# Attention in five batches a unit: a third tile of maxima in the banks of the products with v, and moved copies, squares and statistics

## Chip, cores and metric

The kernel runs on one core of a Trainium2 chip. The metric is the device time of one execution in microseconds (us). TensorE (PE in the profile, PEld for its weight loads), VectorE (DVE), ScalarE (ACT), GpSimd (POOL) and SyncE (SP, which here only issues DMAs) each work through a queue of their own and wait for each other through semaphores. Products land in PSUM, 8 banks of 128 x 512 f32.

## What is computed

```
xn = layernorm(x)                                   # x: 2048 x 512
q, k, v = split(xn @ wqkv)                          # 32 heads of 16
scores = q k^T * 16**-0.5, where 0 <= i - j < 256, else -1e9
s = (softmax(scores) v) @ wo                        # 512 x 512
g = silu((silu(xn @ w1) * (xn @ w3)) @ w2)          # w1, w3: 512 x 1792, w2: 1792 x 512
out = x + s * g
```

All data are f32. The large products are made from f16 halves, high and low, in three products each (high high, high low, low high), so each operand must first be scaled by a power of two and cut in two.

## The kernel before

**Work.** Tokens go in four tiles of 512 (`t`), heads in four groups of eight (`g`). A *unit* is four heads of one group in one tile: 4 x 4 x 2 = 32 units, in the order of `t`, `g`, `p`. The dense work, `gate_up` (L839) and `down` (L884) over 14 slices of the feed-forward weights for each tile, projections of q and k (L534), values (L504) and the final product with wo (`total`, L926), is cut into pieces of mostly 6 matmuls of 128 x 128 x 512.

**Attention.** For each unit `pass1` (L572) makes 8 tiles of scores whose row maxima are reduced on VectorE (products L588, reduction L600). It runs two units ahead, because the maxima, turned by two small products (L615), go out through DRAM into two extra rows of q (L623, L625). `pass2` (L641) makes the scores again, transposed and with the maxima taken off: 4 chunks a unit in the first tile of tokens (`FIRST`), 5 in the others (`CHUNKS`). A chunk is 8 to 12 small products (L662) into a tile `s` of two banks, one or more additions of a mask on VectorE (L669), and one exponential on ScalarE (L672) into a tile `pt`, of which there are four buffers. `values` multiplies chunks with v into the tile `po` (L690). After the last chunk `finish` reads `po` out with a ScalarE copy (L700) and a VectorE addition (L703), and sends the halves out by DMA; the second unit of a pair calls `normalise` (L723): reciprocals go through DRAM, `invert` multiplies on GpSimd, `cut` copies on ScalarE (L743) and subtracts on GpSimd. All small products of attention use quarters or eighths of TensorE side by side.

**PSUM.** Two banks are `m0`, `m1` for dense work, four are two tiles `s` (pool `pss`), two are the one tile `po` (pool `pso`).

**Order.** TensorE runs in the order of the program, written out by hand. The other engines' order is made by the framework from priorities and a model of time. `batches` (L1025) takes a unit's tiles alternately from `pass2` and `pass1`, two to a *batch*, an odd one carried to the next unit; the products with v of a chunk group (`cuts`) are issued at the end of the batch after the one with its last scores (`late`). `spread` (L1063) issues a batch, then dense pieces until their share of the unit's cost is reached; a group of products with v counts as `COLS` = 2.5 matmuls a chunk. `step` counts batches and dense pieces; `later(n, f)` places `f` n steps on. `besides` are small extra products (sums of squares for the scales, transposes of the next x) that ride on a tile of maxima, at most one or two a batch; `beside_scores(n, f)` queues one.

**Preparation.** Weights are read as f32, their squares summed (`squares`, L222: ScalarE L231 or VectorE L233) and cast (L243), summed over partitions by `powers` on TensorE, then cut: `split` (L293) uses a ScalarE copy (L294) and a VectorE subtraction (L295), `split_pool` (L302) two ScalarE copies (L303, L304) and two halves of a GpSimd subtraction (L300). `measure` (L773) does this for two slices of the feed-forward weights, `weights` (L311) for wv and wo. `prepare_beside` (L478) loads the next x, takes its statistics (L406, L407), the reciprocal root (`rstd`) and centres it.

Of the kernel before, what the change touches and what calls it, by code (L numbers as in the profile page):

```python
# [21 lines left out]
P = 128  # L22
# [56 lines left out]
def tile_block(ctx: ExitStack, tc: tile.TileContext, x, wqkv, wo, w1, w3, w2, out):  # L79
# [59 lines left out]
    def later(n, f):  # L139
        made_so_far[0] += 1  # L140
        queue.append((now[0] + n, made_so_far[0], f))
# [80 lines left out]
    def squares(parts, on_act=0, apart=0):  # L222


        ssq = small.tile([P, len(parts)], F32, name="ssq")

        def one(i, raw):

            sq = ppool.tile([P, D], BF16, name="sqa" if i < on_act else "junk", bufs=1)
            if i < on_act:  # L230
                nc.scalar.activation(sq, raw, AF.Square, accum_out=ssq[:, i:i + 1])  # L231
            else:
                nc.vector.tensor_tensor_reduce(out=sq, in0=raw, in1=raw, scale=1.0, scalar=0.0,  # L233
                                               op0=ALU.mult, op1=ALU.add, accum_out=ssq[:, i:i + 1])
        for i, raw in enumerate(parts):
            if apart:
                later(apart * (i // 2 + 1), lambda i=i, raw=raw: one(i, raw))
            else:
                one(i, raw)
        sb = small.tile([P, len(parts)], BF16, name="sb")  # L240

        def cast():
            nc.vector.tensor_copy(sb, ssq)  # L243
        if apart:
            later(apart * (len(parts) + 1) // 2, cast)
        else:
            cast()
        return sb
# [62 lines left out]
    def weights(name, w):  # L311

        cell = {}

        def load():
            cell["raw"] = [take(F32) for _ in range(NC)]
            for c, raw in enumerate(cell["raw"]):
                nc.sync.dma_start(raw, w[c * P:(c + 1) * P, :])

        def norm(apart=0):  # L320
            cell["sb"] = squares(cell["raw"], on_act=2 * (name == "wv"), apart=apart)

        def scale(s=None):
            p2 = const.tile([P, 1], F32, name=f"p2{name}")
            inv = const.tile([P, 1], F32, name=f"inv{name}")

            def rest():
                cell["p2"], cell["inv"], cell["sw"] = p2, inv, scaled(inv, WS, f"sw{name}")
            return then(s, powers(cell["sb"], 1, p2, inv, s), rest)

        def cut(apart=0):
            if name == "wo":

                made = [take(F16) for _ in range(NC)]
                hi, lo = ([m[:, k * D:(k + 1) * D] for m in made] for k in range(2))
            else:
                both = [const.tile([P, NC, D], F16, name=f"{name}{k}") for k in "hl"]
                hi, lo = ([b[:, c, :] for c in range(NC)] for b in both)

            def one(c, raw):  # L340
                split(hi[c], lo[c], raw, cell["sw"])
                give(raw)
            for c, raw in enumerate(cell["raw"]):
                if apart:
                    later(apart * c, lambda c=c, raw=raw: one(c, raw))
                else:
# [131 lines left out]
    def prepare_beside(t, more=0):  # L478


        load, stats, rstd, centre, turn = prepare(t)
        made = [(0, lambda b=b: load(b)) for b in range(4)]
        for b in range(4):
            made.append((0, lambda b=b: later(more + 8 + b, lambda: stats(b))))
        made.append((0, lambda: later(more + 12, lambda: rstd(0, 4))))
        for b in range(4):
            made.append((0, lambda b=b: later(more + 13 + b, lambda: centre(b))))
        return made, lambda: besides.extend(lambda s, b=b, n=n: turn(b, n, s) for b in range(4) for n in (0, 2))

    def value(j, scores_bank=False):  # L490
# [81 lines left out]
    def pass1(t, g, p):  # L572
# [3 lines left out]
        whole = NM[(2 * (t * NG + g) + p) % len(NM)]  # L576
        nm = whole[:, 0:32].rearrange("p (b i) -> p b i", b=2)

        def part(ii, a):
            qa, ka = QA[t, g], keys(t, g)  # L580
            i = t * 4 + ii
            n, mask = ((i + 1) * P, M1.rearrange("p a b -> p (a b)")[:, (1 - i) * P:]) if i < 2 else (WIN, MW)
            s = scores_bank()
            for c in range(2):
                e = (ii + 3) * P if i < 2 else (ii + 2) * P + 64 * (c + 1)
                for r in range(2):
# [24 lines left out]
        def finish(s):  # L611
# [13 lines left out]
                    nc.sync.dma_start(qa[64 * r + KR:64 * r + KR + 2, 2 * p:2 * p + 2, :].rearrange("p a q -> p (a q)"),  # L625
                                      dm.rearrange("(b r i) q -> r b (i q)", b=2, r=2)[r])
            return rest
        return [lambda ii=ii, a=a: part(ii, a) for ii in range(4) for a in range(2)]

    def last_maxima():  # L630
        s = scores_bank()
# [6 lines left out]
    OT = {}  # L638
    ON = {}

    def pass2(t, g, p, cuts):  # L641

        es = WQK[g][2]
        cell = {}
# [70 lines left out]
            values(*cs)  # L715
            finish()
        n = len(chunks)
        cols = [None] * n
        for cs in cuts:
            cols[cs[-1]] = len(cs), lambda cs=cs: (last if cs[-1] == n - 1 else values)(*cs)  # L720
        return [lambda c=c: scores(c) for c in range(n)], cols

    def normalise(t, g):  # L723
        on, dd = ON.pop((t, g))
        dr = small.tile([P, 32], F32, name="dr")
        nc.sync.dma_start(dr, dd.rearrange("h (b c) -> (h b) c", c=32))
# [12 lines left out]

        def cut():  # L740
            OT[t, g] = made = take(F16)
            O[t, g] = o = made.rearrange("p (a q) -> p a q", a=2)
            nc.scalar.copy(o[:, 0, :], on)  # L743
            halves(nc.gpsimd.tensor_sub, o[:, 1, :], on, o[:, 0, :])
        later(8, invert)
        later(18, cut)

# [25 lines left out]
    def measure(f, apart=0):  # L773
# [25 lines left out]
                for k in range(2):  # L799
                    later((1, 2, 4, 6)[2 * i + k], lambda i=i, k=k: cut(i, k))  # L800
        if started:
            beside_scores(4, scale)
        else:
            later(9 if apart else 6, scale)

    def measure_down(k):

# [154 lines left out]
    def feed_forward():  # L962
# [3 lines left out]
        for t in range(NT):  # L966
            for f in range(FB):
                if t == 0:
                    if f % 2 or f == 0:
                        pieces += [(0, lambda f=f: load(0, f)) for f in (range(f + LEAD, min(f + LEAD + 2, FB)) if f else range(4, LEAD + 1))]  # L970
                    elif 0 < f < FB - 2:
                        pieces.append((0, lambda f=f + 2: measure(f, 1)))
                    pieces += [(0, lambda k=k: measure_down(k)) for k, (_, f1) in enumerate(GROUPS) if f == f1 - 1]
                else:
                    if f == 0:
# [42 lines left out]
            done[0] += made[-1][0]  # L1018
        return made

    late = []
    late_cost = [0]
    carried = []

    def batches(n, u, ahead):  # L1025


        rows1 = pass1(*ahead) if ahead else []
        rows2, cols2 = [], []
        if u:  # L1030
            cuts = ((0, 1), (2, 3)) if u[0] == 0 else ((0, 1, 2), (3, 4)) if ahead else ((0, 1), (2, 3), (4,))
            rows2, cols2 = pass2(*u, cuts)
        order = carried[:]
        carried.clear()
        if u and not ahead and maxima:
            order.append((last_maxima, None, 1))
        for k in range(max(len(rows1), len(rows2))):
            order += [(f, c, 0) for f, c in zip(rows2[k:k + 1], cols2[k:k + 1])]
            order += [(f, None, 1) for f in rows1[k:k + 1]]
        if len(order) % 2 and n < len(units) - 1:  # L1040
            carried.append(order.pop())
        pairs = [order[k:k + 2] for k in range(0, len(order), 2)]
        made = []
        due = late_cost[0]
        for pair in pairs:

            pair.sort(key=lambda x: x[2])

            def batch(pair=pair):
                alone[0] = True  # L1050
                for f, _, _ in pair:
                    f()
                ready = late[:]
                late.clear()
                late.extend(c[1] for _, c, _ in pair if c)
                for c in ready:
                    c()
            made.append((due, batch))
            due = sum(COLS * c[0] for _, c, _ in pair if c)
        late_cost[0] = due  # L1060
        return made

    def spread(made, dense):  # L1063
# [136 lines left out]
    want = EARLY  # L1200
    for n, u in enumerate(units):
        if n == 1:
            first, second = prepare_beside(1, 6)
            run(first)
            later(26, second)
        if n == 6:
# [10 lines left out]
        k = n // 2 + 2  # L1217
        if n % 2 == 0 and k < len(tiles):
            later(1, lambda k=k: fetch(*tiles[k]))
    while late:  # L1220
        ready = late[:]
        late[:] = []
        for c in ready:
            c()
        step()
    for b in range(2):
        residual(NT - 1, b)
    run(ffn)
# [31 lines left out]
```

## Time and profile before

| | |
|---|---|
| median of 3 runs | 875.03 us (872.63 to 876.66) |
| the profiled execution | 873.85 us |
| its span, first to last instruction | 872.1 us |
| mean granted TensorE clock | 0.988 |
| TensorE busy | 833.8 us |
| VectorE busy | 607.7 us |
| ScalarE busy | 407.4 us |
| GpSimd busy | 192.4 us |

A row of a group reads: line, engine, operation, tile written <- tiles read, shapes, count, busy time, mean ns of one, idle time before them and what ended most of it. A row of the order of time reads: start, length, engine, line, operation, tiles, shapes, count, and in brackets the idle time of the engine before it with what ended it. Matmuls overlap and their ends are modelled, so intervals between their starts say more than their lengths.

### The profile page before, as it was taken

The page shows a single profiled execution, that of the slowest core. Times are in us where ns is not written, and L with a number is a line of the kernel's source. Part 1 is how long each engine was busy: PE and PEld are TensorE (multiplying, and loading weights), DVE is VectorE, ACT ScalarE, POOL GpSimd, SP SyncE. Part 2 cuts the span into 40 slices and gives each one's busy share as a digit, 9 for nine tenths or more (in the row PEclk, how much of TensorE's full clock was granted, in tenths as well). Part 3 has the DMA queues.
Part 4 walks back from the last instruction along what each step waited for, and adds up shares of the span by engine and source line. Part 5 has one row for each costly group of instructions (what it writes and reads, how often), then busy time and mean ns, then how long its engine had stood idle before and what let it go on. Part 6 is the DMA issues. An engine that isn't in the chain of part 4 may idle for free.

```text
span 872.1 us, 22496 instructions
## 1 busy us (share of the span) xinstructions
PE 833.8 (96%) x8734; PEld 376.8 (43%) x8734; DVE 607.7 (70%) x2017; ACT 407.4 (47%) x594; POOL 192.4 (22%) x317
## 2 busy tenths in 40 slices
PE   9898989979999999999999999999999999999997
PEld 4343434434444444444444444444444444444443
DVE  8686767946797667796768775777676776566435
ACT  6897967372424444334343444343434444342521
POOL 2254338160111203111111211121111113131211
PEclk9999999998999999999999999999999999999999
DMA  9967625335633434452433344344443263433102
GB/s 290 280 209 237 206 81 161 110 108 142 200 107 89 129 95 125 115 171 78 137 106 92 123 112 131 117 116 105 128 128 94 69 152 87 130 94 101 49 9 61
DMA packets 95323, 110.62 MB, mean 127 GB/s; under 512 B 17200, under 2 KB 60528, under 8 KB 95216
## 3 DMA queue, kind: packets, MB, share of 16 engines
q1 hardware_dynamic: 94928, 108.67, 42.6%
q8 instruction: 68, 1.11, 0.6%
q10 hardware_dynamic: 288, 0.52, 0.2%
q14 instruction: 39, 0.32, 0.1%
HBM read 76.28 MB, written 28.57 MB: 120 GB/s over the span
## 4 chain that ended last, share of the span: by engine, by line
PE 71%; DVE 11%; ACT 6%; DMA 5%; issue 4%; POOL 1%; SPq 1%; POOLq 0%; ACTq 0%; DVEq 0%
PE m L839 26%; PE m L884 13%; PE po L690 8%; PE m L534 7%; PE s L662 5%; PE s L588 4%; PE m L504 4%; PE m L926 4%; DVE junk L600 3%; ACT pt L672 2%; DVE s L669 2%; DMA slot<-in_B_w_dram 1%; ACT slot L303 1%; DMA dQ<-slot 1%; ACT sqa L231 1%
## 5 line engine op out<-in xcount | busy, mean ns | idle before, releaser
L672 ACT ACTIVATE pt<-s,es 128x1024 f32<-128x1024 f32 x152 | 168.7, 1112 | 225.6 <-DVE s L669 208.8
L839 PE MATMUL m<-XH,slot 128*128 128x512 f16 x896 | 267.7, 380 | 0.4 <-DVE slot L854 0.2
L300 POOL TENSOR_TENSOR slot<-slot,slot 128x256 f16<-128x256 f32 (+1 forms) x220 | 144.0, 680 | 518.1 <-ACT slot L863 381.5
L600 DVE CUSTOM_DVE_ANT_0 junk<-s,MW 128x320 bf16<-128x320 f32 x448 | 217.3, 485 | 33.6 <-PE s L588 21.0
L839 PEld LDWEIGHTS <-slot 128*128 128x128 f16 x1344 | 123.0, 98 | 154.4 <-issue 15.6
L669 DVE TENSOR_TENSOR s<-s,MK 128x256 f32<-128x256 f32 (+2 forms) x280 | 121.3, 435 | 73.5 <-PE s L662 70.5
L839 PE MATMUL m<-XL,slot 128*128 128x512 f16 x448 | 169.8, 379 | 0.0
L884 PE MATMUL m<-slot,slot 128*128 128x512 f16 x672 | 158.2, 384 | 2.3 <-DVE slot L854 2.0
L884 PEld LDWEIGHTS <-slot 128*128 128x128 f16 x672 | 62.0, 98 | 81.5 <-issue 12.2
L588 PE MATMUL s<-KA,qa 48*64 48x320 f16 (+2 forms) x1024 | 73.2, 299 | 23.4 <-ACT pt L672 13.4
L690 PE MATMUL po<-pt,V 64*32 64x320 f32 (+4 forms) x2880 | 87.0, 350 | 0.0
L662 PE MATMUL s<-qa,KA 50*64 50x320 f16 (+3 forms) x1472 | 62.2, 261 | 3.2 <-DVE M L600 1.6
L690 PEld LDWEIGHTS po<-pt,V 64*32 64x32 f32 x2880 | 48.2, 107 | 29.9 <-issue 9.4
L662 PEld LDWEIGHTS <-KA 50*64 50x64 f16 x1472 | 31.7, 105 | 67.5 <-issue 42.4
L863 ACT CAST slot<-slot 128x512 f16<-128x512 f32 x56 | 34.5, 616 | 53.5 <-DVE slot L859 53.1
L850 ACT ACTIVATE slot<-m,sgs 128x512 f32<-128x512 f32 x56 | 38.2, 683 | 45.0 <-PE m L839 43.7
L854 DVE SCALAR_TENSOR_TENSOR slot<-slot,m 128x512 f32<-128x512 f32 x56 | 38.3, 684 | 27.5 <-ACT slot L850 27.0
L859 DVE SCALAR_TENSOR_TENSOR slot<-m,slot 128x512 f32<-128x512 f32 x56 | 38.5, 687 | 21.5 <-PE m L839 21.3
L588 PEld LDWEIGHTS <-qa 48*64 48x64 f16 x1024 | 29.2, 106 | 53.6 <-issue 29.1
L300 POOL TENSOR_TENSOR on<-on,rb 128x256 f32<-128x256 f32 x32 | 22.6, 727 | 129.2 <-DMA dm<-mt 40.7
L900 DVE SCALAR_TENSOR_TENSOR slot<-m,dsc,slot 128x512 f32<-128x512 f32 x48 | 35.8, 746 | 18.4 <-PE m L884 18.0
L534 PE MATMUL m<-XH,whi 128*128 128x512 f16 x120 | 45.6, 388 | 0.0
(143 smaller groups left out, 832.6 us busy)
## 6 DMA issues: line engine op xcount, KB each, us to landing
slot<-dW SPq DMA_DIRECT2D x126, 256.0 KB
slot<-in_B_w_dram SPq DMA_DIRECT2D x42, 256.0 KB
dW<-slot SPq DMA_DIRECT2D x42, 256.0 KB
slot<-in_A_x_dram SPq DMA_DIRECT2D x30, 256.0 KB
KA<-dK SPq DMA_DIRECT2D x24, 288.0 KB
qa<-dQ SPq DMA_DIRECT2D x32, 192.0 KB
dK<-slot SPq DMA_DIRECT2D x16, 256.0 KB
dQ<-slot SPq DMA_DIRECT2D x16, 256.0 KB
```

The source lines that it names most:

```text
L300: op(out[:, c], a[:, c], b[:, c])
L534: nc.tensor.matmul(cell["pp"], a[:, k, c, :], b[:, c, :], start=(c, i) == parts[0][0], stop=(c, i) == parts[-1][-1])
L588: nc.tensor.matmul(s[64 * c:64 * c + 64, r, :n], qa[rows, 2 * p + a, ii * P + 64 * c:ii * P + 64 * c + 64], ka[rows, 2 * p + a, e - n:e], ...
L600: nc.vector.tensor_tensor_reduce(out=junk[:, :n], in0=s[:, r, :n], in1=mask, scale=1.0, scalar=NEG, op0=ALU.add, op1=ALU.max, accum_out=M[ ...
L662: nc.tensor.matmul(s[64 * h:64 * h + 64, r, o:o + 64 * n], ka[rows, 2 * p + a, 64 * (m + 4):64 * (m + 5)], qa[rows, 2 * p + a, 64 * (m + k ...
L669: nc.vector.tensor_add(v, v, MK[:, kind, of:of + n, :].unsqueeze(1).to_broadcast([P, 2 * len(which), n, 64]))
L672: nc.scalar.activation(pt, s, AF.Exp, scale=es)
L690: nc.tensor.matmul(cell["po"][32 * i:32 * i + 32, h, 64 * (m + k):64 * (m + k + n)], V[64 * h:64 * h + 64, (4 * t + m // 2) % VB, hd * VW: ...
L839: nc.tensor.matmul(cell[k], w[:, (a * NC + c) * P:(a * NC + c + 1) * P], b[:, c, :], start=c == 0 and i == 0, stop=c == NC - 1 and i == 2)
L854: nc.vector.scalar_tensor_tensor(sg, sg, 1.0, cell[0], op0=ALU.add, op1=ALU.mult)
L859: nc.vector.scalar_tensor_tensor(sg, cell[1], 0.5 * HS / (WS * XS)**2, sg, op0=ALU.mult, op1=ALU.mult)
L884: nc.tensor.matmul(ps, hh[:, a * TW + b * P:a * TW + (b + 1) * P], w[:, c * D:(c + 1) * D], start=f == f0 and i == 0, stop=f == f1 - 1 and ...
```

## The change

- `batches` no longer pairs tiles. A written plan gives each unit its batches: `W` is a chunk of scores, `M` a tile of maxima in a tile `s`, `X` a tile of maxima in the two banks of `po`, `L` the turning of the last maxima. A batch holds two or three tiles, and a unit has five batches, two units ahead of the first have three, the last two units four. The products with v of the chunks named in the plan are issued at the end of that same batch; `late` and the carrying go.
- `pass1`'s parts take a flag that puts their tile into `po`.
- From the second tile of tokens on, the plan scores all five chunks before the first products with v.
- `squares` places one square every `apart` steps in place of two, and the cast behind all of them.
- wo is cut by `split_pool`. Statistics of the next x stand two steps apart (one before), `rstd` and centring three steps later; for the second tile all of this starts three steps earlier. The cut of a finished head group stands 24 steps on in place of 18. In the first tile `measure` of two slices is called one slice earlier, its sums ride 8 steps on (4 before).

```diff
@@ squares
-                later(apart * (i // 2 + 1), lambda i=i, raw=raw: one(i, raw))
+                later(apart * (i + 1), lambda i=i, raw=raw: one(i, raw))
...
-            later(apart * (len(parts) + 1) // 2, cast)
+            later(apart * (len(parts) + 1), cast)
@@ weights
-                split(hi[c], lo[c], raw, cell["sw"])
+                (split_pool if name == "wo" else split)(hi[c], lo[c], raw, cell["sw"])
@@ prepare_beside
-            made.append((0, lambda b=b: later(more + 8 + b, lambda: stats(b))))
-        made.append((0, lambda: later(more + 12, lambda: rstd(0, 4))))
+            made.append((0, lambda b=b: later(more + 8 + 2 * b, lambda: stats(b))))
+        made.append((0, lambda: later(more + 15, lambda: rstd(0, 4))))
         for b in range(4):
-            made.append((0, lambda b=b: later(more + 13 + b, lambda: centre(b))))
+            made.append((0, lambda b=b: later(more + 16 + b, lambda: centre(b))))
@@ pass1
-        def part(ii, a):
+        def part(ii, a, beside):
...
-            s = scores_bank()
+            s = pso.tile([P, 2, TW], F32, name="po") if beside else scores_bank()
@@ pass2
-    def pass2(t, g, p, cuts):
+    def pass2(t, g, p):
...
-        cols = [None] * n
-        for cs in cuts:
-            cols[cs[-1]] = len(cs), lambda cs=cs: (last if cs[-1] == n - 1 else values)(*cs)
-        return [lambda c=c: scores(c) for c in range(n)], cols
+        return [lambda c=c: scores(c) for c in range(n)], lambda *cs: (last if cs[-1] == n - 1 else values)(*cs)
@@ normalise
-        later(18, cut)
+        later(24, cut)
@@ measure
-            beside_scores(4, scale)
+            beside_scores(8, scale)
         else:
-            later(9 if apart else 6, scale)
+            later(10 if apart else 6, scale)
@@ feed_forward
-                    elif 0 < f < FB - 2:
-                        pieces.append((0, lambda f=f + 2: measure(f, 1)))
+                    if f % 2 and f + 3 < FB:
+                        pieces.append((0, lambda f=f + 3: measure(f, 1)))
@@ batches
+    FIRST_PLAN = (("WMX", ()), ("WMX", ()), ("WMX", ()), ("WM", (0, 1)), ("M", (2, 3)))
+    PLAN = (("WMX", ()), ("WMX", ()), ("WWX", ()), ("WM", (0, 1, 2)), ("MM", (3, 4)))
+    AHEAD_PLAN = (("MMX", ()), ("MMX", ()), ("MM", ()))
+    LAST_PLANS = ((("LW", ()), ("WW", ()), ("WW", (0, 1, 2)), ("", (3, 4))),
+                  (("WW", ()), ("WW", ()), ("W", (0, 1, 2)), ("", (3, 4))))
...
+        plan = AHEAD_PLAN if not u else LAST_PLANS[n - len(units) + 2] if not ahead else PLAN if u[0] else FIRST_PLAN
+        for kinds, cs in plan:
...
+            def batch(rows=rows, cs=cs):
                 alone[0] = True
+                for f in rows:
                     f()
+                if cs:
+                    cols(*cs)
+            made.append((COLS * len(cs), batch))
@@ the units' loop
-            first, second = prepare_beside(1, 6)
+            first, second = prepare_beside(1, 3)
```

More of the change, by code (lines that the diff above doesn't have):

```diff
@@ L627, in finish @@
             return rest
-        return [lambda ii=ii, a=a: part(ii, a) for ii in range(4) for a in range(2)]
+        return [lambda beside, ii=ii, a=a: part(ii, a, beside) for ii in range(4) for a in range(2)]
     def last_maxima():
@@ L1019, in more @@
         return made
-    late = []
-    late_cost = [0]
-    carried = []
+    FIRST_PLAN = (("WMX", ()), ("WMX", ()), ("WMX", ()), ("WM", (0, 1)), ("M", (2, 3)))
[3 more added lines that the diff above has]
+                  (("WW", ()), ("WW", ()), ("W", (0, 1, 2)), ("", (3, 4))))
     def batches(n, u, ahead):
         rows1 = pass1(*ahead) if ahead else []
[L1029 to L1042, printed above, removed]
-        made = []
[L1044 to L1049, printed above, removed]
@@ new lines, in batches @@
+        rows2, cols = pass2(*u) if u else ([], None)
+        plan = AHEAD_PLAN if not u else LAST_PLANS[n - len(units) + 2] if not ahead else PLAN if u[0] else FIRST_PLAN
+        made = []
+        for kinds, cs in plan:
+            rows = []
+            for k in kinds:
+                if k == "W":
+                    rows.append(rows2.pop(0))
+                elif k == "L":
+                    rows.append(last_maxima)
+                else:
+                    rows.append(lambda f=rows1.pop(0), k=k: f(k == "X"))
+            def batch(rows=rows, cs=cs):
@@ L1050, in batch @@
                 alone[0] = True
-                for f, _, _ in pair:
+                for f in rows:
                     f()
[L1053 to L1060, printed above, removed]
+                if cs:
+                    cols(*cs)
+            made.append((COLS * len(cs), batch))
@@ L1061, in batches @@
+        assert not rows1 and not rows2
         return made
@@ L1219, in tile_block @@
             later(1, lambda k=k: fetch(*tiles[k]))
[L1220 to L1225, printed above, removed]
     for b in range(2):
```

## The prediction

> **What bounds the kernel now.** I read the page's first two parts first, then who makes TensorE wait, then TensorE's order of time around single batches of attention.
>
> ```profile
> span 872.1 us, 22496 instructions
> PE 833.8 (96%) x8734; PEld 376.8 (43%) x8734; DVE 607.7 (70%) x2017; ACT 407.4 (47%) x594; POOL 192.4 (22%) x317
> PEclk9999999998999999999999999999999999999999
> ...
> 0.00:240.00 240.00, 217.14 (x2000) 97.16 (x2000) 169.90 (x656) 156.27 (x284) 82.81 (x153) 0.96 0.60 184
> 240.00:800.00 560.00, 549.62 (x6193) 248.07 (x6184) 405.21 (x1305) 230.29 (x283) 97.74 (x146) 1.00 0.40 113
> 800.00:873.00 73.00, 67.07 (x553) 31.60 (x551) 32.63 (x58) 20.82 (x27) 11.87 (x18) 1.00 0.15 42
> ```
>
> The last three rows are stretches: length, busy time of PE, PEld, DVE, ACT and POOL, granted clock. TensorE is the bound: 549.62 of 560 us in the middle. Its idle time is 22.9 us before 240, 10.4 us to 800, 5.9 us after. The change removes no product, so it can only win in two places: this idle time, with the clock lost through it, and whatever TensorE pays without being idle. The second is found by comparing starts, since ends of matmuls are modelled.
>
> ```profile
> 511.34 0.38 PE L839 MATMUL m<-XL,slot 128*128 128x512 f16 x1
> 511.65 0.47 PE L588 MATMUL s<-KA,qa 48*64 48x320 f16 x8
> 512.04 0.61 PE L839 MATMUL m<-XH,slot 128*128 128x512 f16 x2
> ...
> 514.00 0.59 PE L839 MATMUL m<-XH,slot 128*128 128x512 f16 x2
> 514.43 0.38 PE L839 MATMUL m<-XL,slot 128*128 128x512 f16 x1
> 514.74 0.41 PE L662 MATMUL s<-qa,KA 50*64 50x256 f16 x8
> 514.98 0.31 PE L588 MATMUL s<-KA,qa 48*64 48x320 f16 x4
> 515.22 0.60 PE L839 MATMUL m<-XH,slot 128*128 128x512 f16 x2
> ```
>
> Two matmuls of 512 columns take 514.43 - 514.00 = 0.43 us, so 0.215 us each, or 0.42 ns a column. The first batch holds two tiles of maxima. From the end of the dense stream (511.34 + 0.215) to its resumption (512.04) it takes 0.485 us. Four small products run side by side, so two tiles are 640 columns, 0.27 us; **0.215 us are overhead of entering and leaving**. The second batch (scores and maxima, 512 + 320 columns, 0.35 us) takes 515.22 - 514.645 = 0.575 us: overhead 0.225 us. So a batch costs about 0.22 us however many tiles it holds, and a third tile adds only its 0.13 us of columns.
>
> **The change part by part.**
>
> *Fewer batches.* Before, each unit's tiles go two by two. The first eight units have 4 score tiles and 8 maxima (6 batches), the next 22 have 5 and 8 (6.5 with the carry), the two ahead of the first have 8 maxima (4 each); the last two take 3 each, and the final products one more: 48 + 143 + 8 + 6 + 1 = 206. After: 30 units of 5, two of 3, two of 4: 164. So 42 fewer, 42 x 0.22 = **-9.2 us**. The count rests on the code; the tiles agree with the page:
>
> ```profile
> L672 ACT ACTIVATE pt<-s,es 128x1024 f32<-128x1024 f32 x152 | 168.7, 1112 | 225.6 <-DVE s L669 208.8
> L588 PE MATMUL s<-KA,qa 48*64 48x320 f16 (+2 forms) x1024 | 73.2, 299 | 23.4 <-ACT pt L672 13.4
> ```
>
> 152 exponentials are 8 x 4 + 24 x 5 score tiles, and 1024 / 4 are 256 maxima. The products with v keep their number of groups, except for one less in each of the last two units, which I cost at nothing; they sit inside batches before and after.
>
> *The third tile in po.* It must wait until po is read out. The waits added, their rows, and what is queued behind:
>
> ```profile
> 503.73 0.42 PE L662 MATMUL s<-qa,KA 50*64 50x320 f16 x12
> 503.98 0.31 PE L588 MATMUL s<-KA,qa 48*64 48x320 f16 x4
> ...
> 506.34 1.11 ACT L672 ACTIVATE pt<-s,es 128x1024 f32<-128x1024 f32 x1 [1.90 <-DVE s L669]
> ...
> 506.15 0.48 DVE L600 CUSTOM_DVE_ANT_0 junk<-s,MW 128x320 bf16<-128x320 f32 x1
> 506.56 0.09 DVE L600 DVE_READ_ACCUMULATOR2_ANT M<- 128x1 f32 x1
> ...
> 508.73 0.29 PE L690 MATMUL po<-pt,V 64*32 64x128 f32 x2
> ...
> 510.25 0.68 DVE L703 TENSOR_TENSOR os<-os,po 128x512 f32<-128x512 f32 x1
> ```
>
> In this batch VectorE is through with the maxima 2.67 us after their products start (506.65 - 503.98), and the exponential ends 3.7 us after the scores start. X adds two reductions, 2 x 0.57 = 1.13 us, so its bank is free about 3.7 us (2.67 + 1.13 - 0.13) after its own product. The planner will put some 17 to 18 dense matmuls into a batch without products with v (about 77 dense ones a unit plus 12.5 of column cost, a fifth each): 18 x 0.215 = 3.9 us, and with the batch's own 0.7 us the next X comes 4.5 us later. Slack 0.8 us. At a unit's change the readout of po (L700, L703) ends 510.93 - 508.73 = 2.2 us after the last product; the next X stands behind 12 dense matmuls and two tiles, 2.6 + 0.5 = 3.1 us. Slack 0.9 us. So I cost the wait at nothing; VectorE's reductions lie beside the dense matmuls. When X does wait, everything on TensorE behind it waits too, because TensorE runs in the program's order.
>
> *A fifth pt tile.* From the ninth unit on, five chunks are scored before the first products with v, and pt has four buffers. The fifth exponential then waits until chunk 0 has been used in the same batch (values of three chunks took 500.87 to 502.33, 1.5 us). Behind it on ScalarE stand tanh and casts; its score bank is wanted by batch five. It ends about 1.5 + 1.1 = 2.6 us after the batch's scores; the bank is wanted after 1.5 + 2.6 + 0.1 = 4.2 us. Cost nothing, slack 1.6 us. If a cast delays it beyond that, TensorE stops for the difference.
>
> ```profile
> 500.87 1.53 PE L690 MATMUL po<-pt,V 64*32 64x256 f32 x48
> 502.33 0.39 PE L534 MATMUL m<-XH,whi 128*128 128x512 f16 x1
> ...
> PE s L588 <- ACT pt L672: 13.4, 12, 5.9
> PE m L926 <- ACT slot L743: 1.0, 1, 1.0
> ```
>
> The last two rows are who TensorE waits for (total, times, longest). In the middle stretch the typical wait is for an exponential that still holds a bank, because only 6 or 12 dense matmuls lie between some batches. With 18 between most, I take 2 of the 10.4 us back (bounds: +10, if every slack above is used up, to -8): **-2 us**.
>
> *The tail.* The last products are now followed by about 17 dense matmuls of the unit and the 84 kept ones, not by the 84 alone, so the last division has 3.6 us more: the wait of L926 for the cast L743 goes, **-1.0 us** (bounds 0 to -1).
>
> *The moved statistics, squares and copies.* These are placed where stops happen today:
>
> ```profile
> 81.67 0.69 DVE L406 BATCH_NORM_STATS2 st<-slot 128x6 f32<-128x512 f32 x1 [1.79 <-DMA slot<-in_A_x_dram]
> 84.67 0.59 PE L884 MATMUL m<-slot,slot 128*128 128x512 f16 x1 [2.03 <-DVE slot L854]
> ...
> 107.15 0.63 ACT L231 ACTIVATE sqa<-slot 128x512 bf16<-128x512 f32 x1 [1.43 <-DMA slot<-in_B_w_dram]
> 111.19 0.30 PE L588 MATMUL s<-KA,qa 48*64 48x256 f16 x4 [2.45 <-ACT pt L672]
> ...
> 194.17 0.62 ACT L743 CAST slot<-on 128x512 f16<-128x512 f32 x1 [4.23 <-POOL on L300]
> 195.86 0.48 PE L588 MATMUL s<-KA,qa 48*64 48x320 f16 x4 [5.89 <-ACT pt L672]
> ...
> 84.70:88.00 3.30, 3.30 (x8) 1.14 (x8) 3.30 (x21) 1.73 (x2) 0.00 (x0) 0.50 0.84 247
> 193.92:200.70 6.78, 4.84 (x43) 1.72 (x43) 3.85 (x11) 2.70 (x4) 1.52 (x3) 0.50 0.35 102
> ```
>
> Each is an engine whose queue holds a moved instruction, not yet ready, ahead of what TensorE needs: statistics of x ahead of the gate's product (2.0 us), squares ahead of an exponential (2.45), the cast of a finished head group, waiting for GpSimd, ahead of an exponential (5.9). The clock falls to half right after, 3.3 us and 6.8 us long in the last two rows, which costs another 1.7 and 3.4 us. After a stop of only 2.03 us it fell too. [...]
>
> If the moves clear the first and the last of these, that is 2.0 + 1.7 + 5.9 + 3.4 = 13 us. I don't count on it:
>
> ```profile
> L231 ACT ACTIVATE sqa<-slot x48: 613/628/637, 6.9 to 111.0; 128x512 bf16<-128x512 f32 x48
> L844 SPq DMA_DIRECT2D dW<-slot x28: 320/415/1457, 39.7 to 204.2; - x28
> ```
>
> The last square runs at 111 us, while the slices whose weights it measures are multiplied up to 204 us (the write of a slice's weights stands right behind its products). So these engines run work as soon as its data and their queue allow, far ahead of its place in the program; a later place only lowers its rank. One step instead of half a step between squares, two instead of one between statistics, 24 instead of 18 before the cast, a measurement one slice earlier but 4 steps longer: each draws the order anew, with the same operations and no DMA of their own, while loads on SP follow as slots come free. Nothing excludes a gain or a loss. Bounds: -13 us (above) to +9.3 us (one more stop like that at 190); I take **-2 us**, nearest to no change, since at least the cast gets a lower rank.
>
> *wo's cut.* Four pairs of a ScalarE copy and a VectorE subtraction become eight ScalarE copies and eight GpSimd halves:
>
> ```profile
> L295 DVE SCALAR_TENSOR_TENSOR slot<-slot,swwo,slot x4: 746/747/752, 272.6 to 275.4; 128x512 f16<-128x512 f32 x4
> L926 PE MATMUL m<-slot,slot x180: 379/379/634, 343.9 to 865.5; 128*128 128x512 f16 x180
> ```
>
> VectorE loses 4 x 0.75 = 3.0 us, ScalarE gains 4 x 0.62 = 2.5 us (a cast of 128x512, as at 194.17 above), GpSimd gets 8 x 0.68 = 5.4 us (page: halves of L300 take 680 ns). wo is first used at 343.9 us, some 70 us later: nothing, unless ScalarE's four more copies delay an exponential there (at most 2.5 us).
>
> **Sum**, against the profiled execution's 873.85 us (span 872.1 and 1.75 around it): 873.85 - 9.2 - 2 - 1 - 2 = 859.65. The runs' median is 875.03, 1.2 us higher, inside their own spread of 4 us. I predict **859.5 us**.
>
> **The rivals.**
> *Stops vanish as well.* The stops at 82 and 190 go with their half clocks, 11 us beyond the 2 already counted: 848 us. For: each has a moved instruction in front. Against: work runs far ahead of its place anyway.
> *New stops take the gain.* One stop like that at 190 more (5.9 + 3.4 us) in the crowded first 240 us: 859.5 + 2 + 9.3 = 871 us. For: GpSimd and ScalarE are fullest there and wo adds to both. Against: fewer, longer batches leave queues more time.
> *X waits in po, slower than before.* 94 batches hold an X. If VectorE releases po late by 0.3 us on average beyond the slack, TensorE loses 28 us: 859.5 + 28 = 888 us. It turns slower than before from 14.2 / 94 = 0.15 us each. For: VectorE is 72% busy in the middle (405 of 560), and the slack of 0.8 us is about one of its dense operations. Against: the same reductions are spread over the same time. [...]
>
> **How the numbers follow.** Forecast 0.50, vanishing stops 0.18, new stops 0.16, X waiting 0.16. Faster by over 0.5% (about what a measurement of this kernel tells from no change) is below 870.7 us: 0.50 + 0.18 + 0.02 = 0.70. Within: 0.12, most of the new stops. Slower: 0.16 + 0.02 = 0.18. The range runs from 846 (below the vanishing stops) to 880 us (a light case of X waiting); its two outsides hold some 0.05 and 0.13.
>
> **What would show it.** Right: 164 batches, each still with about 0.22 us of overhead; three tiles in 0.7 us; no wait of an X for L600 or L703; no L926 wait for L743. Wrong: rows of TensorE waiting for L600 or L703 that add up to 10 us and more; exponentials held back by values; further stretches at clock 0.50 before 240 us.

## The result and the profile after

The changed kernel takes 860.8 us in the median (859.9 to 861.6) against 873.8 us beside it on the same chip: a ratio of 0.984, 95% interval 0.982 to 0.987. The profiled execution took 861.0 us. Its page begins:

```profile
span 859.2 us, 22511 instructions
...
PE 820.9 (96%) x8734; PEld 380.0 (44%) x8734; DVE 608.3 (71%) x2013; ACT 407.9 (47%) x598; POOL 198.0 (23%) x325
...
PEclk9999899999999999999999999999999999999999
```

TensorE is idle 859.2 - 820.9 = 38.3 us, exactly as before (872.1 - 833.8 = 38.3). All of the gain, 12.9 us, is in TensorE's *busy* time with the same 8734 matmuls. So the gain is not less waiting in sum; what was left are the overhead between matmuls and the clock. In the two traces attention interrupts the stream of dense 128x512 matmuls 206 times before and 165 times after: 41 x 0.225 = 9.2 us. The clock stood at half for 20.5 us before and for 14.2 us after, which is worth another 3 us or so.

To see where it came from, both executions are cut at the same points of the program: the first scores of the first unit, of the ninth and of the 31st. Rows are length, busy time of PE, PEld, DVE, ACT and POOL, clock, DMA. Before:

```profile
0.00:67.00 67.00, 61.14 (x336) 26.20 (x337) 51.40 (x197) 55.45 (x119) 23.37 (x61) 0.97 0.84 259
67.00:275.54 208.54, 190.21 (x2085) 87.19 (x2085) 148.82 (x564) 114.78 (x185) 64.71 (x100) 0.97 0.49 149
275.54:796.01 520.47, 511.42 (x5736) 229.93 (x5736) 372.49 (x1196) 215.21 (x264) 92.47 (x138) 1.00 0.40 113
796.01:872.07 76.06, 71.06 (x579) 33.51 (x578) 35.02 (x63) 21.93 (x28) 11.87 (x18) 1.00 0.16 45
```

After:

```profile
0.00:65.04 65.04, 59.09 (x341) 25.82 (x342) 52.12 (x204) 53.65 (x115) 22.55 (x59) 1.00 0.84 263
65.04:268.32 203.28, 186.95 (x2081) 87.33 (x2080) 147.41 (x559) 116.06 (x190) 68.48 (x106) 0.97 0.52 153
268.32:785.79 517.47, 505.69 (x5740) 234.27 (x5740) 374.62 (x1191) 216.57 (x267) 95.00 (x143) 1.00 0.41 114
785.79:859.24 73.45, 69.17 (x579) 32.58 (x578) 34.12 (x61) 21.59 (x28) 11.99 (x18) 1.00 0.17 44
```

The stages are 2.0, 5.3, 3.0 and 2.6 us shorter. In the third, busy time falls by 5.7 us while idle time *grows* from 9.1 to 11.8 us. Attention interrupts the dense stream 31 times less there (142 and 111) at the same 3.4 us of half clock, so this stage gives 0.19 us for each, a little under 0.22.

The batch itself is as predicted. TensorE's order of time in the changed kernel, a batch of scores, maxima and a third tile in po:

```profile
560.71 0.38 PE L836 MATMUL m<-XL,slot 128*128 128x512 f16 x1
561.02 0.41 PE L662 MATMUL s<-qa,KA 50*64 50x320 f16 x8
561.26 0.31 PE L588 MATMUL s<-KA,qa 48*64 48x320 f16 x4
561.40 0.30 PE L588 MATMUL po<-KA,qa 48*64 48x320 f16 x4
561.64 0.61 PE L836 MATMUL m<-XH,slot 128*128 128x512 f16 x2
```

From the end of the dense stream (560.71 + 0.215) to 561.64 are 0.715 us; its 1152 columns are 0.484 us, so the overhead is 0.23 us for three tiles as it was for two. (L836 is the old L839; later lines have moved up by three.)

What TensorE waits for has changed, though:

```profile
PE po L588 <- DVE os L703: 9.0, 8, 3.8
PE s L588 <- DVE M L600: 3.6, 2, 2.9
PE s L588 <- ACT pt L672: 2.1, 5, 0.7
...
PE po L588 <- DVE XL L472: 1.4, 2, 1.1
PE po L588 <- DVE M L600: 1.2, 2, 0.7
...
PE po L588 <- DVE mt L621: 1.0, 2, 0.7
```

The wait for an exponential that held a bank fell from 13.4 to 2.1 us. In its place the third tile waits in po: 9.0 + 1.4 + 1.2 + 1.0 = 12.6 us, the most of it for L703, the readout of the unit before. The row of L926 waiting for L743 at the end is gone.

### The profile page after: what moved, and what is told of

Its sections match the earlier page's. It is cut to its first block, busy times and chain, and to the rows that moved or that the text cites. A ratio compares the mean times of both kernels' runs of the same rounds, so it can differ in the third digit from the quotient of the medians.

```text
span 859.2 us, 22511 instructions
## 1 busy us (share of the span) xinstructions
PE 820.9 (96%) x8734; PEld 380.0 (44%) x8734; DVE 608.3 (71%) x2013; ACT 407.9 (47%) x598; POOL 198.0 (23%) x325
## 4 chain that ended last, share of the span: by engine, by line
PE 57%; DVE 15%; issue 7%; DMA 7%; ACT 7%; POOL 4%; SPq 3%; DVEq 0%; POOLq 0%; ACTq 0%
PE m L836 20%; PE m L881 12%; PE po L690 6%; PE m L534 6%; DVE junk L600 5%; PE m L923 3%; POOL slot L300 3%; PE s L662 3%; PE m L504 3%; DVE s L669 2%; PE s L588 2%; ACT pt L672 1%; DMA slot<-in_A_x_dram 1%; DMA dr<-dd 1%; SPq L734 1%
## 5 line engine op out<-in xcount | busy, mean ns | idle before, releaser
L300 POOL TENSOR_TENSOR slot<-slot,slot 128x256 f16<-128x256 f32 (+1 forms) x228 | 149.5, 681 | 568.1 <-ACT slot L860 446.2
L836 PE MATMUL m<-XH,slot 128*128 128x512 f16 x896 | 267.5, 380 | 2.7 <-DVE slot L851 1.9
L836 PEld LDWEIGHTS <-slot 128*128 128x128 f16 x1344 | 125.1, 98 | 158.5 <-issue 16.3
L836 PE MATMUL m<-XL,slot 128*128 128x512 f16 x448 | 169.8, 379 | 0.0
L600 DVE CUSTOM_DVE_ANT_0 junk<-s,MW 128x320 bf16<-128x320 f32 x288 | 139.6, 485 | 30.8 <-PE s L588 20.1
L669 DVE TENSOR_TENSOR s<-s,MK 128x256 f32<-128x256 f32 (+2 forms) x280 | 118.8, 434 | 55.3 <-PE s L662 51.1
L881 PEld LDWEIGHTS <-slot 128*128 128x128 f16 x672 | 63.1, 99 | 84.0 <-issue 14.4
L690 PE MATMUL po<-pt,V 64*32 64x320 f32 (+4 forms) x2880 | 84.8, 345 | 1.3 <-ACT pt L672 1.1
L600 DVE CUSTOM_DVE_ANT_0 junk<-po,MW 128x320 bf16<-128x320 f32 x160 | 77.3, 483 | 6.7 <-DVE M L600 0.5
L662 PE MATMUL s<-qa,KA 50*64 50x320 f16 (+3 forms) x1472 | 58.0, 259 | 1.7 <-ACT pt L672 0.9
L847 ACT ACTIVATE slot<-m,sgs 128x512 f32<-128x512 f32 x56 | 38.3, 683 | 41.8 <-PE m L836 39.7
L588 PE MATMUL s<-KA,qa 48*64 48x320 f16 (+2 forms) x648 | 46.5, 299 | 6.5 <-DVE M L600 3.6
L897 DVE SCALAR_TENSOR_TENSOR slot<-m,dsc,slot 128x512 f32<-128x512 f32 x48 | 35.7, 745 | 20.0 <-PE m L881 19.9
```

Of the source, the lines that this page charges most:

```text
L300: op(out[:, c], a[:, c], b[:, c])
L588: nc.tensor.matmul(s[64 * c:64 * c + 64, r, :n], qa[rows, 2 * p + a, ii * P + 64 * c:ii * P + 64 * c + 64], ka[rows, 2 * p + a, e - n:e], ...
L600: nc.vector.tensor_tensor_reduce(out=junk[:, :n], in0=s[:, r, :n], in1=mask, scale=1.0, scalar=NEG, op0=ALU.add, op1=ALU.max, accum_out=M[ ...
L662: nc.tensor.matmul(s[64 * h:64 * h + 64, r, o:o + 64 * n], ka[rows, 2 * p + a, 64 * (m + 4):64 * (m + 5)], qa[rows, 2 * p + a, 64 * (m + k ...
L669: nc.vector.tensor_add(v, v, MK[:, kind, of:of + n, :].unsqueeze(1).to_broadcast([P, 2 * len(which), n, 64]))
L690: nc.tensor.matmul(cell["po"][32 * i:32 * i + 32, h, 64 * (m + k):64 * (m + k + n)], V[64 * h:64 * h + 64, (4 * t + m // 2) % VB, hd * VW: ...
```

## The experiments

Theory A: the gain is the number of batches times 0.22 us, and the moves only redraw the order in the first 270 us. Rival B: the moves made the gain. Rival C: the third place in PSUM made it, not the number of batches.

**moves_only.** The kernel before with every moved constant and wo's cut, without the plan.

```diff
-                later(apart * (i // 2 + 1), lambda i=i, raw=raw: one(i, raw))
+                later(apart * (i + 1), lambda i=i, raw=raw: one(i, raw))
...
-        later(18, cut)
+        later(24, cut)
...
```

> Only the moved copies, squares and statistics, with the two-tile batches of before. Theory A (the gain is 41 to 42 batches fewer at about 0.22 us each, and the moves only redraw the stops): within 6 us of before, ratio 0.993 to 1.007. Rival B (the moves clear stops and their half clocks): 861 to 865 us, ratio 0.985 to 0.990.

Measured 874.9 us, ratio 0.9995 (0.998 to 1.001). B falls: on the kernel before the moves are worth nothing. The stop of 5.9 us at 190 us, which the prediction hoped a later cast might clear, is still there with the cast 24 steps on, and the same cast still stands in front:

```profile
197.04 0.62 ACT L743 CAST slot<-on 128x512 f16<-128x512 f32 x1 [3.61 <-POOL on L300]
198.72 0.48 PE L588 MATMUL s<-KA,qa 48*64 48x320 f16 x4 [4.75 <-ACT pt L672]
```

In none of the twelve kernels with third tiles in po does TensorE stop for more than 0.9 us between 180 and 205 us, wherever the cast stands. So it is the plan that removed this stop.

**plan_only.** The changed kernel with all moved constants and wo's cut as before.

```diff
-                later(apart * (i + 1), lambda i=i, raw=raw: one(i, raw))
+                later(apart * (i // 2 + 1), lambda i=i, raw=raw: one(i, raw))
...
-        later(24, cut)
+        later(18, cut)
...
```

> Only the written plan with the third tile in po; squares, statistics, wo's cut, the head group's cut and the measurements stay as before. Theory A: 859 to 869 us, at least 9 us under before unless a new stop comes in, ratio 0.983 to 0.994. Rival B: within 4 us of before, ratio 0.995 to 1.005.

Measured 851.9 us, ratio 0.974 (0.972 to 0.976): the best of all, below the band of Theory A too, and 9 us *under* the changed kernel. The plan alone makes 22 us; beside the plan, the moves cost 9. Its stages:

```profile
65.84:263.39 197.55, 186.84 (x2085) 87.03 (x2084) 147.67 (x569) 114.65 (x187) 65.64 (x101) 0.98 0.52 157
263.39:778.74 515.35, 505.88 (x5740) 234.34 (x5740) 375.11 (x1192) 214.74 (x264) 92.57 (x138) 1.00 0.41 115
```

The second stage, the units of the first token tile, is 5.7 us shorter than in the changed kernel, and idle time there is 10.7 us in place of 16.3.

**x_apart.** Each third tile a batch of its own, with dense work in front of it, in all three plans that have one.

```diff
-    PLAN = (("WMX", ()), ("WMX", ()), ("WWX", ()), ("WM", (0, 1, 2)), ("MM", (3, 4)))
+    PLAN = (("WM", ()), ("X", ()), ("WM", ()), ("X", ()), ("WW", ()), ("X", ()), ("WM", (0, 1, 2)), ("MM", (3, 4)))
...
```

> The changed kernel, but each third tile is a batch of its own (still in po, still before the same products with v), with dense work ahead of it: 94 more entries into attention. Theory A: 94 x 0.22 = 20.7 us more than the changed kernel, less up to 9 us that the waits of X for po's readout take today: 873 to 882 us, ratio 0.998 to 1.009. Rival C (what helps is the third place in PSUM, longer gaps for the exponentials, not the number of batches): no slower than the changed kernel, 852 to 862 us.

Measured 888.1 us, ratio 1.016 (1.014 to 1.018): 27 us above the changed kernel, beyond A's 12 to 21. TensorE's order of time there:

```profile
605.88 0.38 PE L504 MATMUL m<-wvh,XL 128*128 128x512 f16 x1
606.19 0.33 PE L588 MATMUL po<-KA,qa 48*64 48x320 f16 x4
606.46 0.39 PE L504 MATMUL m<-wvh,XH 128*128 128x512 f16 x1
```

Alone, from the end of the dense stream (605.88 + 0.215) to its resumption, the tile takes 606.46 - 606.095 = 0.365 us. As the third tile it added 0.14 us, 0.715 us above against 0.575 us for the batch of scores and maxima before. The difference, 0.225 us, is the price of a batch. In the trace attention interrupts the dense stream 83 times more often than in the changed kernel (248 and 165; some of the 94 have no dense work between them): 83 x 0.225 = 19 us. The granted clock is 0.983 in place of 0.992, so by 886.2 x 0.017 - 859.2 x 0.008 some 8 us more are lost to it, and idle time grew by another 1.4 us. The three add up to 28 us, 1 more than measured. The clock's share is an estimate: another execution of this kernel with a clock of 0.988 took the same time. The third stage alone gives the price more directly:

```profile
275.80:812.92 537.12, 521.78 (x5739) 230.76 (x5738) 378.70 (x1190) 214.70 (x264) 93.11 (x138) 0.99 0.39 110
```

TensorE is busy 521.78 - 505.69 = 16.1 us longer, with 6.8 us more at half clock, which cost 3.4; the other 12.7 us over 55 more interruptions (166 and 111) are 0.23 us each. C falls as far as the place in PSUM goes: it was kept, and the time went. Its other half, longer gaps for the exponentials, is not tested apart, because the gaps became shorter with the batches: tiles in s wait 11.6 us for L600 and 9.1 us for exponentials here, against 3.6 and 2.1 in the changed kernel.

**first_no_x.** The first eight units with the third tiles in the second and third batch only, so that none stands behind a readout.

```diff
-    FIRST_PLAN = (("WMX", ()), ("WMX", ()), ("WMX", ()), ("WM", (0, 1)), ("M", (2, 3)))
+    FIRST_PLAN = (("WM", ()), ("WMX", ()), ("WMX", ()), ("WM", (0, 1)), ("MM", (2, 3)))
```

> The changed kernel, with the plan of the first eight units as WM, WMX, WMX, WM, MM in place of WMX, WMX, WMX, WM, M: the same number of batches, but no third tile behind the readout of po. If the waits of X for the readout cost what the trace shows in these units (0.6 + 1.4 + 3.8 us before 150 us, with one or two half clocks of 1.7 to 3.4 us behind them): 851 to 857 us, ratio 0.974 to 0.981. If the stop only moves to the next tile that waits for the same blocked ScalarE queue: 859 to 862 us, ratio 0.983 to 0.987.

Measured 857.9 us, ratio 0.981 (0.980 to 0.983): some 3 us, less than hoped, and the intervals of the two ratios overlap. Who waits in it:

```profile
PE s L588 <- ACT pt L672: 5.3, 8, 1.9
PE s L662 <- DVE M L600: 4.8, 2, 4.0
PE po L588 <- DVE os L703: 3.7, 5, 1.5
PE m L881 <- DVE slot L897: 3.0, 1, 3.0
```

The wait for the readout fell from 9.0 to 3.7 us, but other waits stand near the same places: 4.0 us for L600 at 94 us, where the changed kernel had one of 2.9, and 3.0 us for a feed-forward slot (L897) at 153 us, where its third tile had waited 3.8 at 151. Most of the stop moved to other work of the same late engines.

Which move costs the 9 us? Four kernels each undo one in the changed kernel.

**undo_meas**, the feed-forward measurements:

```diff
-                later(apart * (i + 1), lambda i=i, raw=raw: one(i, raw))
+                later(apart * (i // 2 + 1), lambda i=i, raw=raw: one(i, raw))
...
-            beside_scores(8, scale)
+            beside_scores(4, scale)
...
-                    if f % 2 and f + 3 < FB:
-                        pieces.append((0, lambda f=f + 3: measure(f, 1)))
+                    elif 0 < f < FB - 2:
+                        pieces.append((0, lambda f=f + 2: measure(f, 1)))
```

> The changed kernel with the feed-forward measurements as before (two squares a step, cast, 4 steps to the sums, one slice later). The plan alone gave 851.9 us, 9 us under the changed kernel, so some of the moves cost that in stops. Theory D (one move is the cause): if it is this one, 850 to 854 us, ratio 0.972 to 0.977. Theory E (the moves only redraw the order, and each undone one lands somewhere between): 855 to 866 us, without relation to the sum of 9 us. If it has no part: 859 to 862 us.

Measured 856.7 us, ratio 0.982 (0.979 to 0.985): not the cause of all 9 us, as D had it, but some 2 us, and the intervals of the two ratios overlap.

**undo_stats**, the statistics, root and centring:

```diff
-            made.append((0, lambda b=b: later(more + 8 + 2 * b, lambda: stats(b))))
+            made.append((0, lambda b=b: later(more + 8 + b, lambda: stats(b))))
...
```

> The changed kernel with the statistics, root and centring of the next x at their former steps, and 6 steps ahead of the second tile's. Theory D: 850 to 854 us if this is the move that costs, 859 to 862 us if it has no part. Theory E: anywhere from 855 to 866 us. The stop of 3.8 us for the readout of po at 147 us stands next to these statistics and may go or grow with them.

Measured 860.2 us, ratio 0.986 (0.983 to 0.988): no part of it alone.

**undo_wo**:

```diff
-                (split_pool if name == "wo" else split)(hi[c], lo[c], raw, cell["sw"])
+                split(hi[c], lo[c], raw, cell["sw"])
```

> The changed kernel with wo cut by one ScalarE copy and one VectorE subtraction again. wo is cut at about 270 us and all of the large stops lie before 190 us, so no part of the 9 us: 859 to 862 us, ratio 0.983 to 0.987. Theory D would need 850 to 854 us here; theory E allows 855 to 866 us.

Measured 860.4 us, ratio 0.985 (0.983 to 0.988): no part.

**undo_cut**:

```diff
-        later(24, cut)
+        later(18, cut)
```

> The changed kernel with the cut of a finished head group 18 steps on, as before. Theory D: 850 to 854 us if this move costs the 9 us; 859 to 862 us if it has no part; theory E 855 to 866 us. The stop of 5.9 us that the kernel before had at 190 us behind this cut would come back only if the place in the order decides, and then 866 to 872 us.

Measured 859.5 us, ratio 0.984 (0.981 to 0.987): no part, and the stop of 5.9 us at 190 us did not come back.

**undo_meas_stats**, the edits of undo_meas and undo_stats together:

```diff
-            beside_scores(8, scale)
+            beside_scores(4, scale)
...
-            made.append((0, lambda b=b: later(more + 8 + 2 * b, lambda: stats(b))))
+            made.append((0, lambda b=b: later(more + 8 + b, lambda: stats(b))))
...
```

> The changed kernel with both the measurements and the statistics of the next x as before; wo's cut and the cut after 24 steps stay moved. Theory F (the measurements and the statistics together make the 9 us, since both fill ScalarE and VectorE between 80 and 170 us): 850 to 854 us, ratio 0.972 to 0.977. Theory E (every undone move only redraws): 854 to 862 us, without relation to it.

Measured 854.5 us, ratio 0.979 (0.976 to 0.981): at the slow edge of theory F's band. The measurements alone give about 2.3 us (0.9843 to 0.9817 of 874), which by the times alone could be noise; both together give about 5 and all moves 9, which could not. None of the other three moves shows a part of its own.

What the measurements did can be seen in the traces. The changed kernel has stops of 1.9, 2.9 and 3.8 us at 79, 94 and 151 us. With the statistics, wo or the cut undone all three stay within 0.2 us. With the measurements undone, alone or with the statistics, and in plan_only, the first two fall under 0.9 us and the third to 1.5 to 2.1. (Without plan_only's other edits, one or two others of 2.0 to 2.4 us come in.) In the changed kernel, TensorE, ScalarE and VectorE around its longest stop:

```profile
142.97 1.07 PE L690 MATMUL po<-pt,V 64*32 64x320 f32 x32
...
144.81 1.33 ACT L303 ACTIVATE slot<-slot,sw 128x512 f32<-128x512 f32 x2
148.79 0.62 ACT L304 CAST slot<-slot 128x512 f16<-128x512 f32 x1 [2.65 <-POOL slot L300]
149.32 0.72 ACT L303 ACTIVATE slot<-slot,sw 128x512 f32<-128x512 f32 x1
149.94 0.56 ACT L700 COPY os<-po 128x512 f32<-128x512 f32 x1
...
150.54 0.62 DVE L703 TENSOR_TENSOR os<-os,po 128x448 f32<-128x448 f32 x1 [4.88 <-ACT os L700]
...
151.21 0.25 PE L588 MATMUL po<-KA,qa 48*64 48x128 f16 x4 [3.85 <-DVE os L703]
```

The products with v were through at 144.0. The readout's copy L700 could have started then, but it stood behind a weight cast that waited 2.65 us for a slot which GpSimd still used, and came at 149.94. VectorE idled, and the third tile held up all of TensorE. In plan_only the same readout stands less far behind its products:

```profile
137.42 1.07 PE L690 MATMUL po<-pt,V 64*32 64x320 f32 x32
...
142.68 0.56 ACT L700 COPY os<-po 128x512 f32<-128x512 f32 x1
...
143.95 0.25 PE L588 MATMUL po<-KA,qa 48*64 48x128 f16 x4 [2.13 <-DVE os L703]
```

The copy starts 4.2 us after the products there (138.5 to 142.68), and 5.9 us after them in the changed kernel.

**plan_nox.** plan_only with first_no_x's plan.

```diff
-    FIRST_PLAN = (("WMX", ()), ("WMX", ()), ("WMX", ()), ("WM", (0, 1)), ("M", (2, 3)))
+    FIRST_PLAN = (("WM", ()), ("WMX", ()), ("WMX", ()), ("WM", (0, 1)), ("MM", (2, 3)))
```

> The plan alone (no moves), with the first eight units as WM, WMX, WMX, WM, MM. If the 9 us of leaving the moves and the 3 us of leaving the first third tile add up: 848 to 850 us, ratio 0.969 to 0.973. If both took away the same stops (X waiting for the readout of po before 160 us): 850 to 854 us, ratio 0.972 to 0.977.

Measured 857.4 us, ratio 0.982 (0.980 to 0.984): outside both bands, and 5 us *slower* than plan_only (7 by the ratios), clear of noise. What took some 3 us off the changed kernel costs 5 to 7 here. No sum of single effects gives this. TensorE is idle for 16.2 us in the second stage, in plan_only for 10.7, in many stops of 1.0 to 1.7 us for VectorE and ScalarE; why their order came out so was not followed further.

**pt5.** Five buffers for pt, and two slots fewer to make room.

```diff
-SLOTS = 41
+SLOTS = 39
-            cell[c] = pt = ppool.tile([P, 2, 512], F32, name="pt")
+            cell[c] = pt = ppool.tile([P, 2, 512], F32, name="pt", bufs=5)
```

> The changed kernel with five buffers for pt in place of four, so that the fifth exponential of a unit waits for no products; to make room, two of the 41 slots of 2 KB go. By the prediction's step this wait costs nothing: 858 to 863 us, ratio 0.983 to 0.988 (more only if the two slots hold loads back). If it costs 0.3 us a unit in 24 units: 851 to 855 us.

Measured 853.3 us, ratio 0.978 (0.975 to 0.981), as if the wait cost 0.3 us a unit. Its third stage is shorter than in all other kernels with five batches a unit (515 to 520 us, cut at the same points):

```profile
266.28:777.07 510.79, 502.65 (x5741) 233.74 (x5740) 375.13 (x1191) 216.13 (x267) 95.14 (x143) 1.00 0.42 116
```

But the direct sign is missing: the fifth exponential of a unit ends 2.95 us after its scores in the median, with four buffers 2.97. With four buffers, too, ScalarE waits for products with v before an exponential only once, for 0.6 us in all (the changed kernel). So the step of the prediction that put this wait at nothing holds, and the gain of 6 to 7 us does not come from the buffer itself. A part of the difference is the clock, some 1.7 us by estimate: the three stops around 390 us, after which it is at half for 3.4 us in the changed kernel (last section), are here too, but the clock is 1.00 around them. Whether fewer slots changed when loads start is not shown, and what did the rest stays open.

**readout_dve.** The first half of the readout as a VectorE copy.

```diff
-                nc.scalar.copy(os, po[:, 0, :])
+                nc.vector.tensor_copy(os, po[:, 0, :])
```

> The changed kernel with the first half of po's readout as a VectorE copy in place of the ScalarE copy. If X waits for the readout because that copy stands behind blocked casts on ScalarE: the 9.0 us of X waiting for L703 fall to under 4 us and the time to 850 to 857 us, ratio 0.972 to 0.980. If VectorE's own queue is what holds the readout, its 32 more copies of some 0.6 us make it worse: 862 to 872 us, ratio 0.986 to 0.998.

Measured 864.4 us (859.3 to 865.6), ratio 0.989 (0.986 to 0.993). The longest wait of X for L703 fell from 3.8 to 1.5 us, so ScalarE's queue was its cause; but the sum fell only from 9.0 to 7.9 us, and the kernel was not faster: its median is 3.6 us above the changed kernel's, with intervals that just overlap. Taking the work to the fuller engine did not pay here. That the 32 more copies on VectorE cost the difference is not shown: the profiled execution, 859.3 us, was the fastest of its runs, so it does not show where the median's other 5 us lie.

## Why the prediction was right, and where not

**Fewer batches, -9.2 us: right.** I counted 42 fewer, the traces show 41. The price was 0.23 us for a batch of three tiles and 0.225 us for one of a single tile, and a kernel with 83 more entries into attention loses them again at that price.

**The tail, -1 us: right.** The wait of L926 is gone (moves_only still has 0.7 us of it), and idle time in the last stage falls from 5.0 to 4.3 us. The 5.9 us that I read there came from a stretch that ran 0.9 us past the last instruction.

**The middle, -2 us: wrong in sign.** Idle time grew by 2.7 us. The waits for exponentials fell as argued, in the third stage from 5.1 to 2.1 us. (Of the 13.4 us that I showed for them, 9.3 lay before this stage.) But the step "So I cost the wait at nothing" for the third tile in po failed: X waits 4.6 us in this stage, 3.1 of them for L703. I took the readout at 2.2 us from one unit, which was typical of the kernel before; after the change its median in this stage is 2.8 us and its longest 5.9 us, against a room of 3.1 us. So 0.3 us of slack was left for the typical unit, and none for the late ones. The other 8.0 of X's 12.6 us lie before 268 us, where one readout takes 7.5 us. Rows of TensorE waiting for L600 or L703, which I had named as a sign of being wrong from 10 us on, add up to 9.0 + 3.6 + 1.2 + 0.8 = 14.6 us (4.3 before). This is the mechanism of the third rival at 0.13 us for each of 94 tiles; it stayed below the 0.15 us at which I had it turn slower.

**The moves, -2 us: wrong.** Beside the plan they cost 9 us, on the kernel before nothing. The bounds (-13 to +9.3) hold, and no run contradicts the step "a later place only lowers its rank"; "nearest to no change, since at least the cast gets a lower rank" fails, since the cast's place made no difference in either direction. What I had left out is that the moved measurements hold up ScalarE where po's readout stands behind them.

**What made up for it.** The plan alone made 22 us, of which batches and tail explain 10. The other 12 us are fewer stops and half clocks: idle time fell from 38.3 us to 29.3 in plan_only, and the time at half clock from 20.5 to 13.7. Most of it lies before 275 us (idle there 24.2 us before, 16.0 in plan_only), and the largest piece is the stop of 5.9 us at 190 us with its 6.8 us at half clock. I had put such a gain into a rival and credited it to the moves; moves_only shows that they do not bring it. That longer gaps between batches bring it, by giving ScalarE and VectorE time to catch up, is my reading and not shown: x_apart, with shorter gaps, does not have the stop at 190 us either, and plan_nox has plan_only's number of batches and loses a part of the gain. So the sum came out by luck, from two errors that cancel: the plan was worth 22 us and not 12, the moves cost 9 us where I had them gain 2.

## What to carry to other kernels

Where small tiled products alternate with dense ones, count the entries: each cost some 0.2 us here, with one tile or with three, and a third tile beside two others added 0.14 us where its bank was free. The third tile should not wait for a bank that is read out in two hops through a queue full of other work (9.0 us of waiting in the changed kernel, 3.8 us of it in one stop); look at the late cases of that readout and not at the typical one. And undo the small moves that come with a large change one by one and all together: here they hid 9 of 22 us.

## What the runs showed of the hardware

A stop of 2 us did not always halve the clock. In the kernel before it stood at 0.50 over 84.70:88.00, after the stop of 2.03 us at 82 us. In the changed kernel the first two rows below stand for two single stops, with the clock over the stretches around them:

```profile
PE s L258 <- DVE al L273: 2.0, 1, 2.0
...
PE m L881 <- DVE slot L851: 1.9, 1, 1.9
...
36.00:60.00 24.00, 20.38 (x133) 8.63 (x134) 21.13 (x92) 22.36 (x50) 12.86 (x20) 1.00 0.68 223
76.00:93.90 17.90, 13.07 (x144) 5.86 (x141) 15.67 (x60) 13.65 (x28) 7.57 (x12) 1.00 0.85 232
```

After three stops of 0.77, 0.77 and 0.71 us within 3.0 us, however, it stood at half:

```profile
387.93 0.41 PE L662 MATMUL s<-qa,KA 50*64 50x256 f16 x8 [0.77 <-DVE M L600]
389.11 0.33 PE L588 MATMUL s<-KA,qa 48*64 48x320 f16 x4 [0.77 <-DVE M L600]
390.15 0.33 PE L588 MATMUL po<-KA,qa 48*64 48x320 f16 x4 [0.71 <-DVE os L703]
...
391.10:394.40 3.30, 3.30 (x9) 1.21 (x8) 2.35 (x10) 1.11 (x1) 1.14 (x2) 0.50 0.26 75
```

In pt5 the first of the same three stops is even longer, and the clock is 1.00 in the stretches around them:

```profile
383.36 0.41 PE L662 MATMUL s<-qa,KA 50*64 50x256 f16 x8 [1.24 <-DVE M L600]
384.54 0.33 PE L588 MATMUL s<-KA,qa 48*64 48x320 f16 x4 [0.77 <-DVE M L600]
385.58 0.33 PE L588 MATMUL po<-KA,qa 48*64 48x320 f16 x4 [0.71 <-DVE os L703]
...
380.70:384.10 3.40, 1.84 (x15) 0.60 (x13) 3.19 (x11) 0.00 (x0) 0.02 (x1) 1.00 0.30 78
384.10:387.50 3.40, 2.25 (x18) 1.07 (x19) 3.30 (x10) 0.61 (x1) 1.23 (x2) 1.00 0.06 13
```

So neither the longest of the stops nor their sum, 2.25 us in the changed kernel and 2.72 us in pt5, tells the two cases apart; what does is not shown.
